# Opening stretch of a fused delta-rule attention and FFN kernel in a new layout

## The chip, the cores and the metric

One core of a Trainium2 chip. The metric is device time of one launch in microseconds (us), median of several runs. The engines are PE (matmul), DVE (vector), ACT (activations), POOL (general) and SP, which here only issues DMAs.

## What is computed

Two stages, one after the other in the reference:

```python
# attention: 4 batches, 8 heads, 768 tokens, head size 48
for t in range(S):
    kt, vt, bt = (k_n[:, :, t], v[:, :, t], beta[:, :, t, None])   # k_n: normalised k
    y[:, :, t] = np.einsum('bhd,bhde->bhe', q[:, :, t], state)
    v_old = np.einsum('bhde,bhd->bhe', state, kt)
    state = state + bt[:, :, :, None] * np.einsum('bhd,bhe->bhde', kt, vt - v_old)
# FFN on y as 3072 x 384, with w_in 384 x 2048 and w_out 2048 x 384
h = x @ w_in
sp = np.maximum(h, 0.0) + np.log1p(np.exp(-np.abs(h)))
g = h * erf(sp)
return (g @ w_out).astype(np.float32)
```

## The kernel before

**Attention.** Tokens are taken in 12 chunks c of 64. Per chunk: norms of k (norm_sq L197, norm_sum L205, norm_ops), a Gram matrix of k with itself ("pg", gram_mm L259, gram_a L269) and of q with k ("pq", gram_mm, gram_p L278 on ACT or L280 on DVE with the causal mask, gram_p2 L287 on POOL for the mask where gram_p was on ACT). For two chunks together (a pair, six of them) the triangular systems are solved in 32-by-32 blocks: the Gram matrix goes to DRAM (to_dram L294), back as blocks (to_blocks L303), 31 rows of two operations each (solve_row L320, L322; pair 0 on DVE, the others on POOL), then out and back again (put_blocks L327, from_blocks L334, from_blocks2 L342). The blocks are merged into whole inverses: merge_t (L349, DVE transposes), merge_e (L357), merge_e2 (L362), merge_z (L370), merge_z2 (L374), merge_m (L383), merge_m2 (L388 ACT, L390 DVE). The recurrence is a chain of 48 steps j = 4c + batch: load_v (L398), put_v (L405, POOL), chain_u (L418, PE), chain_u2 (L424, DVE), chain_s (L431), chain_s2 (L437 ACT or L439 DVE), chain_y (L445), chain_y2 (L454, ACT), chain_m (L458, DVE).

**FFN.** Four steps j make one of 12 token groups g (256 tokens). x is scaled and split into two fp16 halves (x_max to x_lo, L568 to L610). A group has 16 units: ffn1 (L622, nine matmuls 128x256 in fp16), and ffn2 (L677 to L679, six matmuls 128x384). Between them, two units at a time (u = 0 to 7): e_sp (L644, softplus on ACT), e_erf (L649, ACT), e_mul (L653, DVE), e_split (L660 ACT or L662 DVE), e_rest (L666, DVE or POOL). Softplus and erf have different tables on ACT, and each change is a table load (L139).

**Weights.** w_in and w_out come as float64 and are made into fp16 pairs on the chip, in 12 raw slices of 512 KB each: w_load (L490, SP), w_mask (L496, ACT), w_sign (L503, DVE), w_bits (L509 and L511, DVE), w_sum (L516, ACT), then for all slices w_max, w_all (PE), w_scale, and w_hi (L550, ACT) and w_lo (L559, DVE) in 16 parts each. Raw slices use the rooms ("H" and "L" tags) that the FFN's pairs use later.

**Room and order.** warm and fill (L154) are matmuls 128x384 on zeros: 15 at the start and WU single ones spread over the opening. early() (L122) lends w_out's room to tiles of the first pairs. PSUM: psa is a ring of three banks, pr is three banks, and "ph" and the warms have two. Every engine takes its instructions in order. Each step is put in a list with a planned time (on(), us(x), with constants such as C2, C3, MT, S1, WO that place chains, merges, solves and weights), the list is sorted by it, and then put in the order of ORDER, a tuple of indices written out (L33); so ORDER, not the planned times alone, sets each engine's queue. SP's queue holds loads, blocks and raw slices in one line, POOL's queue holds the solves, put_v, masks and half of e_rest.

Of the kernel before, what the change touches and what calls it, by code (L numbers as in the profile page):

```python
# [14 lines left out]
P = 128  # L15
# [19 lines left out]
MD = 4.4  # L35
CS = 1.2
WARM = 15
C2 = 2.0
C3 = 11.5
SS2 = 12.8  # L40
S1 = -2.5
SPL = 32
WG = -6
WU = 440
MT = 54
M1 = 0
# [36 lines left out]
@with_exitstack
def delta_ffn_kernel(ctx, tc, kT, qT, ktok, vtok, btok, w_in, w_out, cst, out):
# [151 lines left out]
    def norm_ops(sg, i, w=0):  # L236
        if i == 0:
            no[sg, w] = norms(sg, w)
        for fn in no[sg, w][i:i + 1] if sg < NSP else no[sg, w][3 * i:3 * i + 3]:
            fn()  # L240

    def load_kf(c, name):
        if c == 3 and name == "kpg":
            kf = early(5120, 1024).rearrange("p (a x) -> p a x", a=BP)
        else:
            kf = io.tile([P, BP, C], F32, tag="kf", bufs=3, name=f"{name}{c}")
        st[c][name] = kf
        for hb in range(2):
            sp.dma_start(kf[rd(hb)], kT[c, hb])
# [46 lines left out]
    def to_blocks(c):  # L296
        sg, i = divmod(c, 2)
        if i == 0:
            gb_t[sg] = at.tile([P, 32, 32], F32, tag="gb", name=f"gb{sg}") if sg else early(0, 1024).rearrange("p (a b) -> p a b", a=32)
        dv = st[c]["d1"].rearrange("(f s) h a t -> f (h a) s t", f=2)  # L300
        for f in range(2):
            q0 = i * 64 + f * 32
            sp.dma_start(gb_t[sg][q0:q0 + 32], dv[f, :, :, f * 32:f * 32 + 32])  # L303

    def solve_init(sg):
        xb_t[sg] = at.tile([P, 32, 32], F32, tag="xb", name=f"xb{sg}") if sg else early(1024, 1024).rearrange("p (a b) -> p a b", a=32)
        x = xb_t[sg].rearrange("p a b -> p (a b)")
        ge.memset(x, 0.0)
        ge.memset(x[:, ::33], 1.0)
# [426 lines left out]
    for i in range(WU):  # L736
        on(us(6 + 0.12 * i), fill)
# [212 lines left out]
```

## Time and profile before

| | us |
|---|---|
| runs of the kernel: median (lowest to highest of 3) | 709.91 (708.35 to 712.67) |
| the run that was profiled | 712.84 |
| span of the profiled execution | 711.1 |
| PE busy | 669.8 (94%) |
| ACT busy, of it table loads | 543.4 (76%), 237.4 |
| DVE busy | 435.9 (61%) |
| POOL busy | 332.3 (47%) |
| mean granted PE clock | 0.966 |

The span is counted from the first to the last instruction; the time of a run is a little longer. Engines work side by side, and a busy share is a mean over stretches with different limits.

### The profile page before, as it was taken

Reading aid. Unit: us, or ns where it says so; the run is one execution under the profiler, and the core shown is the slowest. Engines: PE = TensorE matmul, PEld = TensorE weight load, DVE = VectorE, ACT = ScalarE, POOL = GpSimd, SP = SyncE. Lnnn points to the kernel's source line nnn. Section 1 sums busy time; section 2 is a strip of 40 time slices with the busy share of each in tenths; the row PEclk is TensorE's granted clock in tenths of the full one; section 3 lists DMA queues with packets and bytes.
Section 4 is the critical chain, followed back from the end, with each engine's and each line's share of the span. In section 5 each row is a group of like instructions: output and inputs, shape, how many; then the busy total and the mean of one; then the engine's idle time right before and its main releaser. Section 6 shows DMA issues by size and latency. Waiting matters only on the chain.

```text
span 711.1 us, 22264 instructions
## 1 busy us (share of the span) xinstructions
PE 669.8 (94%) x9475; PEld 507.0 (71%) x9475; DVE 435.9 (61%) x1000; ACT 543.4 (76%) x767; POOL 332.3 (47%) x500
## 2 busy tenths in 40 slices
PE   7999997468999999999999999999999999999997
PEld 5666675356777787886878777877868777777764
DVE  3699859367896874777745659564564455534321
ACT  6214374378899999995994986967978969879993
POOL 4403999344201797898139751178831223201111
PEclk9999997577999999999999999999999999999999
DMA  9486541770004615713445114432041120000000
GB/s 244 105 257 209 166 126 42 210 173 14 3 2 109 152 38 120 159 42 93 85 91 135 35 33 96 101 81 64 18 97 29 26 63 7 24 1 13 12 23 22
DMA packets 87395, 59.05 MB, mean 83 GB/s; under 512 B 67776, under 2 KB 77120, under 8 KB 87296
## 3 DMA queue, kind: packets, MB, share of 16 engines
q1 hardware_dynamic: 87296, 57.63, 32.8%
q8 instruction: 74, 1.21, 0.7%
q14 instruction: 25, 0.20, 0.1%
HBM read 43.45 MB, written 14.16 MB: 81 GB/s over the span
## 4 chain that ended last, share of the span: by engine, by line
PE 67%; ACT 13%; DVE 5%; DMA 5%; issue 4%; POOL 3%; SPq 1%; POOLq 0%; ACTq 0%; DVEq 0%
PE ph L622 18%; PE warm L154 10%; ACT L139 7%; PE pr L677 6%; PE pr L679 6%; PE pr L678 6%; PE pg L259 3%; PE pc L445 3%; PE pc L418 3%; PE pq L259 2%; PE pm L383 2%; DMA k<-ktok 2%; PE pc L431 2%; ACT L L649 2%; ACT L L644 2%
## 5 line engine op out<-in xcount | busy, mean ns | idle before, releaser
L139 ACT ACT_TABLE_LOAD x185 | 237.4, 1283 | 4.0 <-PEq L943 0.7
L622 PE MATMUL ph<-xh,w_in 128*128 128x256 f16 x1152 | 204.2, 274 | 4.2 <-DVE L L653 3.9
L622 PEld LDWEIGHTS <-w_in 128*128 128x128 f16 x1728 | 165.9, 98 | 32.3 <-DVE L L653 4.4
L666 POOL TENSOR_TENSOR H<-L,H 128x512 f16<-128x512 f32 x58 | 67.0, 1157 | 242.9 <-DVE H L662 154.9
L622 PE MATMUL ph<-xl,w_in 128*128 128x256 f16 x576 | 157.4, 273 | 0.0
L653 DVE SCALAR_TENSOR_TENSOR L<-ph,L 128x512 f32<-128x512 f32 x96 | 66.1, 689 | 114.4 <-ACT L L649 107.6
L677 PE MATMUL pr<-w_out,H 128*128 128x384 f16 x384 | 126.0, 328 | 0.0
L679 PE MATMUL pr<-w_out,H 128*128 128x384 f16 x384 | 125.6, 327 | 0.0
L678 PE MATMUL pr<-w_out,H 128*128 128x384 f16 x384 | 125.6, 327 | 0.0
L320 POOL TENSOR_TENSOR tmptmpg<-gb,xb 128x31 f32<-128x31 f32 (+15 forms) x155 | 88.8, 573 | 51.1 <-DMA gb<-d 42.0
L322 POOL TENSOR_TENSOR xb<-xb,tmptmpg 128x31 f32<-128x31 f32 (+15 forms) x155 | 88.6, 571 | 12.1
L644 ACT ACTIVATE L<-ph,xct 128x512 f32<-128x512 f32 x96 | 65.8, 687 | 21.6 <-POOL z L405 9.1
L154 PE MATMUL warm<-zero 128*128 128x384 f16 x455 | 80.2, 337 | 1.1 <-DVE zero L145 1.1
L405 POOL TENSOR_TENSOR z<-v,nm 64x192 f32<-64x192 f32 x96 | 58.5, 609 | 28.8 <-DMA v<-vtok 22.0
L154 PEld LDWEIGHTS <-zero 128*128 128x128 f16 x455 | 44.6, 100 | 31.8 <-issue 3.6
L649 ACT ACTIVATE L<-L 128x512 f32<-128x512 f32 x96 | 60.4, 629 | 1.1
L679 PEld LDWEIGHTS <-H 128*128 128x128 f16 x384 | 37.7, 98 | 25.1 <-issue 0.3
L677 PEld LDWEIGHTS <-H 128*128 128x128 f16 x384 | 37.6, 98 | 20.8 <-issue 0.2
L678 PEld LDWEIGHTS <-H 128*128 128x128 f16 x384 | 37.7, 98 | 18.6 <-issue 0.2
L666 DVE TENSOR_TENSOR H<-L,H 128x512 f16<-128x512 f32 x38 | 28.1, 740 | 25.9 <-ACT H L660 25.8
L424 DVE TENSOR_TENSOR z<-pc,ga 64x192 f32<-64x192 f32 x88 | 31.2, 355 | 17.7 <-PE pc L418 15.3
L259 PE MATMUL pq<-qp,kpq 48*64 48x64 f32 x640 | 25.4, 238 | 16.8 <-DMA qp<-qT 16.8
(138 smaller groups left out, 961.6 us busy)
## 6 DMA issues: line engine op xcount, KB each, us to landing
raw_in<-w_in SPq DMA_DIRECT2D x12, 512.0 KB, 7.6
raw_out<-w_out SPq DMA_DIRECT2D x12, 512.0 KB, 4.8
d<-A SPq DMA_DIRECT2D x20, 256.0 KB, 3.1
k<-ktok SPq DMA_DIRECT2D x12, 384.0 KB, 4.0
qp<-qT SPq DMA_DIRECT2D x24, 192.0 KB, 3.5
v<-vtok SPq DMA_DIRECT2D x48, 96.0 KB, 2.9
out<-ob SPq DMA_DIRECT2D x48, 96.0 KB, 2.2
kpg<-kT SPq DMA_DIRECT2D x22, 192.0 KB, 5.0
```

Source lines behind the costliest of these rows:

```text
L139: se.add_instruction(mybir.InstLoadActFuncSet(name=nc.get_next_instruction_name(), act_func_set_id=i, ins=[], outs=[]))
L154: te.matmul(wp[0], zero[:, :P], zero, start=True, stop=True)
L320: eng.tensor_tensor(tv, G[:, s, s + 1:].unsqueeze(1).broadcast_to([P, ncol, nr]), Xv[:, :, s:s + 1].broadcast_to([P, ncol, nr]), op=ALU.mult)
L322: eng.tensor_tensor(Xv[:, :, s + 1:], Xv[:, :, s + 1:], tv, op=ALU.add)
L622: te.matmul(ph, w[:, i, kt * P:kt * P + P], G[x][:, :, ksl], start=(m == 0), stop=(m == 8))
L644: se.activation(unit(g, u), G["ph", u], AF.Softplus, bias=0.0, scale=G["ct"])
L649: se.activation(Lu, Lu, AF.Erf, bias=0.0, scale=1.0)
L653: ve.scalar_tensor_tensor(Lu, fg[g]["ph", u], HSC, Lu, op0=ALU.mult, op1=ALU.mult)
L666: (ve if u % (2 if g < GLE else GLM) == 0 else ge).tensor_tensor(G["gl", u], unit(g, u), G["gh", u], op=ALU.subtract)
L677: te.matmul(G["po"][a], gh[:, o, asl], wout_h[:, i, :], start=(i == 0), stop=False)
L678: te.matmul(G["po"][a], gh[:, o, asl], wout_l[:, i, :], start=False, stop=False)
L679: te.matmul(G["po"][a], gl[:, o, asl], wout_h[:, i, :], start=False, stop=(i == NFF - 1))
```

## The change

The work is the same; its place in time and its rooms change.

- The second solve (chunks 2 and 3) is planned from us(76) to us(116) in place of us(30) to S1, and with it go later: loads and norms of the pair, its grams (the second half-gram of chunk 2 stands behind the warms), to_dram. Merges are planned from MT = 58 (54), the chains of chunks 2 and 3 from C2 = 12 (2) and C3 = 16 (11.5).
- w_in's slices 0 to 5 are loaded right behind the first loads, and masked, signed and made into bits ahead of solve 0; slices 6 to 11 within and behind it.
- w_out's slices are planned one by one (WOT): 0 to 3 within solve 0, 6, 10 and 11 next, then 4, 5, 7, 8, 9. Before, all came from WO in steps of 0.4.
- q of chunks 0 and 1 is loaded behind to_blocks; v of the first six steps early.
- WU is 390 (440). In the new order 32 warms stand ahead of the grams of chunk 0, 109 ahead of the pq grams, 235 ahead of half-gram 2 1, one ahead of w_all and merge_e 0, and none later.
- HB, the rooms for pairs and raw slices of tag "H", is 7 (6). The early() rooms of chunk 3's gram input, chunk 3's A, and the first solve's two tiles are gone: they now come from their own pools.
- S2A is empty: chain_s2 of steps 0 to 3 is on DVE (an addition) and not on ACT (a copy). CP and CM are (2, 3): gram_p of chunks 0 and 1 is on DVE with the mask in it (no POOL step), and half of the merge copies of chunks 0 and 1 are on DVE.
- e_split of groups 0 and 1 is all on ACT (before, and in later groups, units 0, 2, 4, 6).
- ORDER is new throughout. On DVE from half-gram 2 1 on: gram_a 2 1, merge_t 0, w_scale, merge_t 1, then w_lo spread between merge copies, gram_p, chain and bit operations, to x_lo 0 1. On PE: merge_e 0 and 1, merge_z 0 and 1, grams 3, chain steps and merge_m of chunk 1, pq grams 2, x_tr, ffn1 0 behind chain_y 6.

```diff
--- before.py
+++ after.py
@@ -30,28 +30,26 @@
 RW = 512
 HALF = BP // 2
 
...
 LEAD = 3
 MD = 4.4
 CS = 1.2
 WARM = 15
-C2 = 2.0
-C3 = 11.5
+C2 = 12.0
+C3 = 16.0
 SS2 = 12.8
 S1 = -2.5
 SPL = 32
 WG = -6
-WU = 440
-MT = 54
+WU = 390
+MT = 58
 M1 = 0
-WL = (1, 25, 25.1, 25.2, 25.3, 25.4, 25.5, 25.6, 26, 26.1, 26.2, 26.3)
-WK = (14, 27, 28, 29, 30, 31, 32, 33, 34, 35, 36, 37)
-WF = (14.5, 42.02, 42.03, 42.04, 42.05, 42.06, 43, 44, 45, 46, 47, 48)
-WI = (20, 47.2, 48.2, 49.4, 52, 54, 56, 58, 60, 62, 64, 66)
-WO = -4.1
+WL = (0.9, 0.95, 1.0, 1.05, 1.1, 1.15, 24, 24.1, 31.0, 32.5, 34.0, 35.5)
+WK = (6.0, 6.7, 7.4, 8.1, 8.8, 9.5, 28, 29, 36.0, 37.5, 39.0, 40.5)
+WF = (6.6, 7.3, 8.0, 8.7, 9.4, 10.1, 28.6, 29.6, 36.6, 38.1, 39.6, 41.1)
+WI = (17.0, 18.0, 19.0, 20.0, 21.0, 22.0, 31, 32, 50.5, 52.1, 53.7, 55.3)
+WOT = (36, 38, 40, 42, 76, 78, 62, 86, 88, 90, 72, 74)
 WD = 0.4
-SGI = ()
-SGO = ()
 RI = "HLHLHLHLHLHH"
 RO = "H" * 12
 LMI = [0] * 16
@@ -60,7 +58,7 @@
 LOD = 0.25
 SPA = (0, 2, 4, 6)
 EB = 2
-HB, LB = 6, 5
+HB, LB = 7, 5
 GLE = 7
 GLM = 4
 PA, PB = 3, 3
@@ -68,9 +66,9 @@
 NSP = 0
 XR = 3
 YR = 6
-S2A = (0, 1, 2, 3)
-CP = (0, 1, 2, 3)
-CM = (0,1,2,3)
+S2A = ()
+CP = (2, 3)
+CM = (2, 3)
 FB = 6.9
 T0 = 82.0
 SW = 4.6
@@ -190,7 +188,7 @@
 
     def norm_sq(c):
         s = st[c]
-        if c < 4:
+        if c < 2:
             s["sq"] = ff.tile([P, BP, D], F32, tag="L", bufs=LB, name=f"sq{c}")
         else:
             s["sq"] = at.tile([P, BP, C], F32, tag="A", name=f"sq{c}")[:, :, :D]
@@ -236,14 +234,11 @@
     def norm_ops(sg, i, w=0):
         if i == 0:
             no[sg, w] = norms(sg, w)
-        for fn in no[sg, w][i:i + 1] if sg < NSP else no[sg, w][3 * i:3 * i + 3]:
+        for fn in no[sg, w][3 * i:3 * i + 3]:
             fn()
 
     def load_kf(c, name):
-        if c == 3 and name == "kpg":
-            kf = early(5120, 1024).rearrange("p (a x) -> p a x", a=BP)
-        else:
-            kf = io.tile([P, BP, C], F32, tag="kf", bufs=3, name=f"{name}{c}")
+        kf = io.tile([P, BP, C], F32, tag="kf", bufs=3, name=f"{name}{c}")
         st[c][name] = kf
         for hb in range(2):
             sp.dma_start(kf[rd(hb)], kT[c, hb])
@@ -261,8 +256,8 @@
     def gram_a(c, i):
         s = st[c]
         if i == 0:
-            if c in (1, 3):
-                s["A"] = early(1024 * (1 + (c + 1) // 2), 1024).rearrange("p (a x) -> p a x", a=BP)
+            if c == 1:
+                s["A"] = early(2048, 1024).rearrange("p (a x) -> p a x", a=BP)
             else:
                 s["A"] = at.tile([P, BP, C], F32, tag="A", name=f"A{c}")
         hs = slice(i * HALF, i * HALF + HALF)
@@ -296,14 +291,14 @@
     def to_blocks(c):
         sg, i = divmod(c, 2)
         if i == 0:
-            gb_t[sg] = at.tile([P, 32, 32], F32, tag="gb", name=f"gb{sg}") if sg else early(0, 1024).rearrange("p (a b) -> p a b", a=32)
+            gb_t[sg] = at.tile([P, 32, 32], F32, tag="gb", name=f"gb{sg}")
         dv = st[c]["d1"].rearrange("(f s) h a t -> f (h a) s t", f=2)
         for f in range(2):
             q0 = i * 64 + f * 32
             sp.dma_start(gb_t[sg][q0:q0 + 32], dv[f, :, :, f * 32:f * 32 + 32])
 
     def solve_init(sg):
-        xb_t[sg] = at.tile([P, 32, 32], F32, tag="xb", name=f"xb{sg}") if sg else early(1024, 1024).rearrange("p (a b) -> p a b", a=32)
+        xb_t[sg] = at.tile([P, 32, 32], F32, tag="xb", name=f"xb{sg}")
         x = xb_t[sg].rearrange("p a b -> p (a b)")
         ge.memset(x, 0.0)
         ge.memset(x[:, ::33], 1.0)
@@ -497,10 +492,7 @@
 
     def w_sign(nm, i):
         hi = wt[nm]["raw", i][:, :, 1]
-        if i in (SGI if nm == "in" else SGO):
-            ge.tensor_scalar(hi, hi.bitcast(F32), 0.0, -2.0 ** 31, op0=ALU.is_lt, op1=ALU.mult)
-        else:
-            ve.tensor_scalar(hi, hi, -0x80000000, None, op0=ALU.bitwise_and)
+        ve.tensor_scalar(hi, hi, -0x80000000, None, op0=ALU.bitwise_and)
 
     def w_bits(nm, i, k):
         raw = wt[nm]["raw", i]
@@ -656,7 +648,7 @@
         G = fg[g]
         pr_ = pair(g, u)
         G["gh", u], G["gl", u] = pr_[:, 0], pr_[:, 1]
-        if (g * NFF // EU + u) % 8 in SPA:
+        if g < 2 or u in SPA:
             se.copy(G["gh", u], unit(g, u))
         else:
             ve.tensor_copy(G["gh", u], unit(g, u))
@@ -708,8 +700,8 @@
         return chain_at(c * B) - MD * (0.65 if c == 2 else 1) if c > 1 else us(MT)
 
     NSG = NC_ // 2
-    solve_end = [us(42), S1] + [chain_at(2 * sg * B) - MD - 1.3 for sg in range(2, NSG)]
-    solve_start = [us(22), us(30), SS2] + [solve_end[sg - 1] + 1.3 for sg in range(3, NSG)]
+    solve_end = [us(50), us(116)] + [chain_at(2 * sg * B) - MD - 1.3 for sg in range(2, NSG)]
+    solve_start = [us(28), us(76), SS2] + [solve_end[sg - 1] + 1.3 for sg in range(3, NSG)]
 
     def gram(t, d, c, name):
 
@@ -734,17 +726,19 @@
     on(-99, clear_second)
     on(-98, warm, WARM)
     for i in range(WU):
-        on(us(6 + 0.12 * i), fill)
+        on(us(6 + 0.17 * i), fill)
     on(us(0), clear_q)
-    for i, (fn, *a) in enumerate(((load_step, 0), (load_step, 1), (load_beta, 0), (load_kf, 0, "kpg"), (load_kf, 1, "kpg"), (load_q, 0), (load_q, 1),
+    for i, (fn, *a) in enumerate(((load_step, 0), (load_step, 1), (load_beta, 0), (load_kf, 0, "kpg"), (load_kf, 1, "kpg"),
                                   (load_cst,))):
         on(us(0.1 + 0.05 * i), fn, *a)
     on(us(6.5), clear_x)
+    on(us(19), load_q, 0)
+    on(us(21), load_q, 1)
     for sg in range(2):
-        t = (4, 10.5)[sg]
+        t = (4, 20)[sg]
         if sg:
             for i, (fn, a) in enumerate(((load_step, 2), (load_step, 3), (load_beta, 1))):
-                on(us(0.6 + 0.05 * i), fn, a)
+                on(us(14 + 0.05 * i), fn, a)
         for x in range(2):
             on(us(t + 1.1 * x), norm_sq, 2 * sg + x)
             on(us(t + 1.1 * x + (0.2 if sg == 0 else 1.0)), norm_sum, 2 * sg + x)
@@ -754,25 +748,24 @@
                     on(us(5.5 + 0.9 * w + 0.22 * i), norm_ops, sg, i, w)
         else:
             for i in range(6):
-                on(us((6.4, 13.4)[sg] + 0.4 * i), norm_ops, sg, i)
+                on(us((6.4, 24)[sg] + 0.3 * i), norm_ops, sg, i)
     for c in range(4):
-        t = (5.5, 8, 12.2, 15)[c]
-        ta = (10.6, 12, 16.3, 18)[c]
+        t = (5.5, 8, 63.2, 65.2)[c]
+        ta = (10.6, 12, 64, 66)[c]
         for i in range(2):
             on(us(t + 1.3 * i), gram_mm, c, i, "pg")
             on(us(ta + 0.6 * i), gram_a, c, i)
-        on(us((11.9, 13.3, 17.6, 19.3)[c]), to_dram, c)
+        on(us((11.9, 13.3, 66, 68)[c]), to_dram, c)
     on(us(14), to_blocks, 0)
     on(us(14.1), to_blocks, 1)
     on(us(1), solve_init, 0)
-    on(us(0.8), load_kf, 2, "kpg")
-    on(us(0.85), load_kf, 3, "kpg")
+    on(us(30), load_kf, 2, "kpg")
+    on(us(30.5), load_kf, 3, "kpg")
     for c in range(2):
         for i in range(2):
-            t = 20.8 + 2.5 * (2 * c + i)
+            t = (56, 57, 71.5, 73)[2 * c + i]
             on(us(t), gram_mm, c, i, "pq")
-            on(us(t + 2.6), gram_p, c, i)
-            on(us(24.6 + 2.5 * (2 * c + i)), gram_p2, c, i)
+            on(us((64, 65, 72.7, 74.2)[2 * c + i]), gram_p, c, i)
 
     for sg in range(NSG):
         t0, t1 = solve_start[sg], solve_end[sg]
@@ -807,8 +800,8 @@
                     on(tq + 0.6 + 0.9 * i, gram_p2, c, i)
         else:
             tm = [us(MT + x + 1.25 * c) for x in (0, 1.2, 2.2, 3.6, 4.8, 6, 7.2, 7.3, 8.5)]
-            on(us(22 + c), from_blocks, c)
-            on(us(42.4 + 0.2 * c), from_blocks2, c)
+            on(us(30 + c), from_blocks, c)
+            on(us(50.4 + 0.2 * c), from_blocks2, c)
             if c == 1:
                 tm = [us(MT + M1 + x) for x in (1.2, 2.4, 3.4, 4.8, 6, 10.5, 11.7, 11.8, 13)]
         on(tm[0], merge_t, c)
@@ -826,8 +819,8 @@
     for j in range(B * NC_):
         t = chain_at(j)
         d = 1.0 if j >= 2 * B else 2.6 / SW / CS
-        on(t - 3.3 if j >= 2 * B else t - us(4) + us(0), load_v, j)
-        on(t - 1.2 if j >= 2 * B else t - us(2) + us(0), put_v, j)
+        on(t - 3.3 if j >= 2 * B else us(32 + 2 * j) if j < 6 else t - us(6) + us(0), load_v, j)
+        on(t - 1.2 if j >= 2 * B else us(52 + 1.3 * j) if j < 6 else t - us(2) + us(0), put_v, j)
         on(t, chain_u, j)
         on(t + 0.2 * d, chain_u2, j)
         if j < B * NC_ - B:
@@ -846,14 +839,14 @@
             on(us(tb + 0.8 * k), w_bits, "in", i, k)
         on(us(tb + 2.4), w_sum, "in", i)
     for i in range(NRW):
-        t = WO + WD * i
+        t = us(WOT[i])
         on(t - 0.9, w_load, "out", w_out.bitcast(I32), i, RO[i])
         on(t - 0.3, w_mask, "out", i)
         on(t - 0.2, w_sign, "out", i)
         for k in range(2):
             on(t + 0.15 * k, w_bits, "out", i, k)
         on(t + 0.5, w_sum, "out", i)
-    for nm, t in (("in", us(WI[-1] + 3)), ("out", WO + WD * (NRW - 1) + 1.2)):
+    for nm, t in (("in", us(WI[-1] + 3)), ("out", us(max(WOT)) + 1.2)):
         on(t, w_max, nm)
         on(t + 0.05, w_all, nm)
         on(t + 0.15, w_scale, nm)
```

## Rows read from the trace of the kernel before

**Rows 1.** Busy time by stretch; PEclk is PE's granted clock.
```profile
core 0: us, PE busy (x) PEld busy (x) DVE busy (x) ACT busy (x) POOL busy (x), PEclk, DMA share, GB/s
...
84.00:115.00 31.00, 29.67 (x675) 21.80 (x674) 20.73 (x40) 21.30 (x50) 28.83 (x35) 1.00 0.42 119
115.00:145.00 30.00, 16.55 (x220) 13.43 (x216) 15.92 (x44) 13.29 (x27) 17.39 (x27) 0.60 0.57 147
...
75.00:125.00 50.00, 45.19 (x806) 31.99 (x803) 39.03 (x82) 28.49 (x68) 45.95 (x60) 0.92 0.36 109
...
289.00:711.00 422.00, 412.45 (x5941) 317.10 (x5934) 231.03 (x529) 346.01 (x446) 183.70 (x289) 1.00 0.24 55
```

**Rows 2.** Timeline of PE (start, duration, line, tiles, count, idle before).
```profile
10.75 3.32 PE L154 MATMUL warm<-zero 128*128 128x384 f16 x11
...
37.35 46.65 PE L154 MATMUL warm<-zero 128*128 128x384 f16 x286
83.93 1.20 PE L357 MATMUL pe<-T,A 32*32 32x32 f32 x64
...
99.13 0.67 PE L418 MATMUL pr<-z,xm 128*64 128x48 f32 x16
...
119.44 1.09 PE L418 MATMUL pc<-z,xm 128*64 128x48 f32 x16 [0.59 <-DVE xm L575]
...
134.94 4.12 PE L259 MATMUL pq<-qp,kpq 48*64 48x64 f32 x64 [10.59 <-DMA qp<-qT]
...
162.25 0.28 PE L622 MATMUL ph<-xh,w_in 128*128 128x256 f16 x1
...
163.47 0.38 PE L622 MATMUL ph<-xh,w_in 128*128 128x256 f16 x2
```

**Rows 3.** Timeline of DVE in the opening stretch.
```profile
38.08 0.18 DVE L320 TENSOR_TENSOR tmpT<-w_out 128x31 f32<-128x31 f32 x1
...
53.01 0.68 DVE L509 SCALAR_TENSOR_TENSOR w_in<-w_in,raw_in 128x512 int32<-128x512 int32 x1
53.61 0.40 DVE L320 TENSOR_TENSOR tmpT<-w_out 128x240 f32<-128x240 f32 x1
...
75.87 1.43 DVE L349 STREAM_TRANSPOSE T<-xm 32x512 f32<-32x512 f32 x2
...
123.78 1.08 DVE L610 SCALAR_TENSOR_TENSOR xl<-pt,xsx,xh 128x256 f16<-128x256 f32 x3
```

**Rows 4.** Instructions by line and form on DVE: count, busy us, mean ns.
```profile
L424 DVE TENSOR_TENSOR z<-pc,ga 64x192 f32<-64x192 f32 x88 | 31.2, 355 | 17.7 <-PE pc L418 15.3
...
L280 DVE TENSOR_TENSOR qp<-pq,mask 64x512 f32<-64x512 f32 x32 | 22.0, 688 | 3.3 <-PE pq L259 2.7
...
L559 DVE SCALAR_TENSOR_TENSOR w_in<-w_in,sc_in 128x384 f16<-128x384 f32 x16 | 10.3, 641 | 17.1 <-ACT w_in L550 16.9
```

**Rows 5.** Timeline of SP's DMA queue.
```profile
66.12 1.09 SPq L327 DMA_DIRECT2D d<-w_out  x2
...
126.19 1.09 SPq L327 DMA_DIRECT2D d<-xb  x2
```

**Rows 6.** Timeline of POOL: first and last operation of two solves.
```profile
64.28 0.48 POOL L320 TENSOR_TENSOR tmptmpg<-gb,xb 128x31 f32<-128x31 f32 x1 [37.37 <-DMA gb<-d]
...
125.90 0.27 POOL L322 TENSOR_TENSOR xb<-xb,tmptmpg 128x31 f32<-128x31 f32 x1
...
233.29 0.24 POOL L320 TENSOR_TENSOR tmptmpg<-gb,xb 128x31 f32<-128x31 f32 x1 [1.83 <-DMA gb<-d]
...
274.95 0.27 POOL L322 TENSOR_TENSOR xb<-xb,tmptmpg 128x31 f32<-128x31 f32 x1
```

**Rows 7.** Timeline of ACT: table load and two softplus.
```profile
140.94 1.28 ACT L139 ACT_TABLE_LOAD   x1
142.24 0.69 ACT L644 ACTIVATE L<-ph,xct 128x512 f32<-128x512 f32 x1
...
289.13 0.69 ACT L644 ACTIVATE L<-ph,xct 128x512 f32<-128x512 f32 x1
```

2 lines of the change are left out of this document (1 added, 1 removed).

## Prediction

> **What bounds the kernel now.** I read four views in this order: the busy table by stretch, TensorE's (PE's) timeline, then the timelines of the engines that release it, and last the two softplus instructions that cut the run into parts.
>
> By stretches [rows 1]: from 289 us on PE is busy 412.45 of 422 us at clock 1.00, so 59% of the span is PE work and falls only if PE has less left to do. The stretch 115 to 145 is the weak one: PE 16.55 of 30 us, DVE 15.92, ACT 13.29, POOL 17.39, granted clock 0.60. Nobody is full there.
>
> PE's timeline [rows 2]: 286 warm matmuls fill 37.35 to 84.0 (0.163 us each), and the merge of chunk 0 follows at once at 83.93. A full engine here is a wait in disguise: the first solve on DVE starts at 38.08 [rows 3], and its blocks go out at 66.12 [rows 5]. At 134.94 PE has waited 10.59 us for a load of q. That load is queued on SP behind the put_blocks at 126.19 [rows 5], which wait for the second solve on POOL, 64.28 to 126.17 (the first and the last of 62 operations, [rows 6]). So a POOL solve holds up a load that has nothing to do with it. The first softplus, at 142.24, is the end of the opening stretch; the first of group 3, at 289.13, is where PE becomes the bound [rows 7].
>
> I cut the time at those two: opening 142.2, middle 146.9, rest 421.9 (711.1 minus 289.13). The run that was profiled took 712.84, so 1.7 lie around the span, and it is 0.4% above the median, 709.91. I sum in its frame and scale at the end.
>
> **Opening, to the merge of chunk 0.** Only the norms and grams of chunks 0 and 1 stand ahead of solve 0 now, but 12 bit operations for w_in slices 0 to 5, six w_sign, and the second pair's norms (18 short operations) do too. The list ahead of the solve ends at about 36, near the 38.08 of before [rows 3]. The solve itself carries 22 weight operations (10 w_sign, 12 w_bits; before: 19), so it ends at about 70 to 72.5, and merge_t could follow 10 us later as before (blocks put at 66.12, merge_t at 75.87 [rows 3, 5]), at 80 to 82. PE is later than that. Eleven warms at 10.75 took 3.32 us at the lower clock [rows 2]; 32 of them and three grams end near 20.7 (an estimate, 18 to 24). Then 109 x 0.163 = 17.8, the four pq grams 3.9, seven warms 1.1, one gram 1.0, 235 x 0.163 = 38.3: 82.8. Only then comes gram 2 1, and DVE's gram_a 2 1 waits for it, with both merge_t queued behind. So merge_t 0 is at 84.6 and merge_e 0 at about 86.5, against 83.93. Fewer warms (390 for 440) buy nothing here: the loss is 2.5, and if solve 0 ends later than 72.5 it is that which counts.
>
> **Opening, from there to the first softplus.** DVE holds the list: from gram_a 2 1 to x_lo 0 1 about 101 instructions. 16 w_lo at 0.641 are 10.3; 15 of 512 columns (3 gram_a; 6 gram_p of chunks 0 and 1, now with the mask on DVE; 6 merge copies, now half on DVE) at 0.688 are 10.3; 32 of the chain (14 chain_u2, 12 chain_s2, of which 8 come from ACT, 6 chain_m) at 0.355 are 11.4 [rows 4]; 10 w_bits at 0.68 are 6.8; 6 x_lo are 2.2 [rows 3]; 4 transposes and 5 w_sign, bounded by 0.688, 6.2; 13 small ones at 0.2, 2.6. Together 49.8. Starts follow one another up to 0.08 before the end of the instruction ahead (53.01 plus 0.68, next at 53.61 [rows 3]), so 42 at least; I take 45. The waits are the unknown: before, 75 to 125 held the same kind of work with 39.03 of 50 busy [rows 1], 11 of wait; I take 10. From 83.9: 138.9. Two ffn1 units and the table load stand between x_lo and softplus: 3.2, as from 139.06 to 142.24. First softplus at **142.1**, where it was. The 10.59 of before are gone (chunk 2's q is loaded long before solve 1 ends), but the w_lo, gram_p and bit work that lay beside them is now in line.
>
> The cost of no warms is in this too: after merge_e 0 the new order has none. A chain_u took 0.67 among warms (99.13) and 1.09 without (119.44) [rows 2]. PE's work to the first ffn1 is about 25 us at full clock, 50 at half, in a stretch of 53: hidden if it alternates well with DVE, and not if it doesn't.
>
> The Trainium skill, "TensorE: Matmul & The Clock Gate", section "A second HAM failure mode: psum-queue depth-cycling", describes PE pausing between bursts while it cycles through PSUM banks and so falling back to the lower clock, at a cost in throughput. The trace agrees: 0.60 in 115 to 145, where there are no warms, and 1.00 in 84 to 115, where there are [rows 1]. By that rule the stretch would run at the 1.2 GHz level, which is the first rival below.
>
> **Middle, first softplus to group 3's.** I sum PE and ACT in the new order between the softplus of units 0 0, 0 4, 1 0, 2 0 and 3 0, with ffn1 at nine times 0.111 (162.25 to 163.47, 11 matmuls), ffn2 at six times 0.163, and a table load of 1.28 at each change [rows 2, 7]. The larger of the two: ACT 26, ACT 20.5, PE 57 (chains 8 to 15 and four merge_m moved here, ACT 50), ACT 39.5, together 143. Before by the same sums: 38, 25, 39, 34, 136, which took 146.9, so 11 of stalls. The 57 is 16 ffn1 (16.0), 16 ffn2 (15.7), eight chain steps at 1.69 (13.5), five grams (4.9), four merge_m (3.8), a merge_e and a merge_z (2.2) and the transposes of x (1.2). The eight e_split that come to ACT in groups 0 and 1 are in ACT's sums. Stalls that I see: load_q 3 waits for chain_y 7, and gram 3 0 pq for it ahead of ffn1 4, about 4. Solve 1 now starts at about 115: by the second solve of before it takes 61.9, by the third 41.9 (233.29 to 275.22) [rows 6]; I take 52, and 12 more to the merge, 179. PE is at merge_e 2 near 185, so no stall, but 4 late by the long price. Solve 2 against merge_e 4: 0 to 4. I take 8: 151.
>
> **Rest.** At that softplus PE is 9 us further in the new order: 3 ffn2 units (2.9), two chain_u and one chain_s and chain_y (2.3), a merge_e and a merge_z (2.2), two merge_m (1.9). In a stretch that is PE's own this is worth its full 9: 421.9 - 9.3 = 412.6. The seventh H room only covers a wait for a room; split work of ACT against DVE is off the path here.
>
> **Sum.** 142.1 + 151 + 412.6 = 705.7; with 1.7, 707.4; times 709.91/712.84, **704.5**.
>
> **Rivals.**
> - *Half clock takes the opening* (slower). PE at its lower level and the three PSUM banks make DVE wait at every chain step. The row for it: 115 to 145, without warms, DVE share 0.53 [rows 1]. By it 45/0.53 = 85, first softplus 172, sum 736, run 734. It decides as soon as DVE's share falls under about 0.66 (45/0.66 = 68 for 55), which is also just the 0.67 of 84 to 115, a stretch with warms. Against it: in 115 to 145 a third of the stretch is the one wait for q, which goes.
> - *The gain is given back* (no change). Solve 1 goes at the slow price and merge_e 2 comes 4 late, or the 57 of PE in group 1 is at less than full clock; 5 more: 709.
> - *DVE hardly waits* (more gain). w_lo and w_bits are spread through the list so that DVE always has work: 4 of wait, softplus at 134 to 136, stalls 4: 693.
>
> **How the numbers follow.** Forecast as summed, 698 to 710: 0.42. Hardly any wait, 686 to 698: 0.19. Given back, 706 to 714: 0.17. Half clock, 714 to 736: 0.22. About 1% is what a measurement can tell from no change: under 702.8 is faster, over 717.0 slower. Faster: all of the third rival and half of the forecast's 0.42, 0.40. Slower: nearly all of the first rival, 0.21. Within 1%: 0.39. Range 688 to 722, which leaves out the worst half of the half-clock case and the best end of the other; the forecast alone is 698 to 710.
>
> **What would show it.** gram_a 2 1 on DVE waiting for PE near 84 shows the opening right. DVE busy at least 0.8 from there to x_lo 0 1, and a softplus at 140 to 144, show the list; a share under 0.66 with a clock near 0.5 to 0.6 shows the first rival. No wait of PE for q before ffn1. In the middle, a first merge_e 2 that follows ffn1 without a wait shows solve 1 in time. From group 3's first softplus to the end 412 to 413, if PE is that much further; a rest of 422 would make that step wrong.

## The result

The changed kernel takes 705.82 us (median of 13 runs, 702.92 to 706.95), the kernel before 712.24 in the same comparison (13 runs, 707.75 to 713.52): a ratio of 0.9908, with an interval of 0.9887 to 0.9928. The forecast was 704.5 against 709.91, a ratio of 0.9924. The profiled execution has a span of 704.9 for 711.1.

Busy time by stretch of the kernel after: merge of chunk 0 to x_lo, then between the first softplus of groups 0, 1, 2 and 3, then to the end (answering to [rows 1]).

```profile
core 0: us, PE busy (x) PEld busy (x) DVE busy (x) ACT busy (x) POOL busy (x), PEclk, DMA share, GB/s
...
85.00:137.10 52.10, 36.44 (x798) 33.00 (x798) 44.85 (x102) 28.24 (x57) 17.00 (x25) 0.64 0.67 174
...
140.70:190.50 49.80, 42.95 (x561) 33.21 (x561) 42.31 (x84) 45.28 (x69) 42.86 (x59) 0.90 0.23 51
...
190.50:249.30 58.80, 57.95 (x1041) 45.14 (x1040) 40.60 (x99) 48.78 (x74) 40.16 (x69) 1.00 0.33 76
...
249.30:289.90 40.60, 40.39 (x560) 30.89 (x559) 25.11 (x50) 39.11 (x50) 24.05 (x46) 1.00 0.63 136
...
289.90:704.90 415.00, 405.64 (x5731) 313.49 (x5729) 227.98 (x518) 348.07 (x443) 171.93 (x268) 1.00 0.23 51
```

The same view of the kernel before, its last stretch from its first softplus of group 3:

```profile
285.20:711.10 425.90, 416.25 (x6002) 320.10 (x5999) 232.90 (x532) 349.76 (x449) 186.95 (x297) 1.00 0.24 56
```

Timeline of PE after ([rows 2]): the long block of warms, half-gram 2 1, merge_e 0, the first ffn1, merge_e 2.

```profile
45.52 38.36 PE L152 MATMUL warm<-zero 128*128 128x384 f16 x235
...
83.81 1.15 PE L254 MATMUL pg<-kpg 48*64 48x64 f32 x32
...
87.41 1.20 PE L352 MATMUL pe<-T,A 32*32 32x32 f32 x64 [1.17 <-DVE m_in L520]
...
137.00 0.40 PE L614 MATMUL ph<-xh,w_in 128*128 128x256 f16 x1
...
184.68 1.20 PE L352 MATMUL pe<-T,A 32*32 32x32 f32 x64
```

Timeline of DVE after ([rows 3]): first and last operation of solve 0, gram_a 2 1, merge_t 0, x_lo 0 1.

```profile
37.41 0.19 DVE L315 TENSOR_TENSOR tmpT<-gb,xb 128x31 f32<-128x31 f32 x1
...
75.02 0.22 DVE L317 TENSOR_TENSOR xb<-xb,tmpT 128x31 f32<-128x31 f32 x1
...
85.00 0.69 DVE L264 TENSOR_TENSOR A<-pg,gn 128x512 f32<-128x512 f32 x1 [2.37 <-PE pg L254]
...
85.61 1.42 DVE L344 STREAM_TRANSPOSE T<-xm 32x512 f32<-32x512 f32 x2
...
135.98 1.08 DVE L602 SCALAR_TENSOR_TENSOR xl<-pt,xsx,xh 128x256 f16<-128x256 f32 x3
```

SP's queue ([rows 5]): put_blocks of solve 0, from_blocks2, load_q 2, put_blocks of solve 1. Load_q 2 stands 55.6 us ahead of the put_blocks that it stood behind.

```profile
75.26 1.09 SPq L322 DMA_DIRECT2D d<-xb  x2
...
78.36 4.51 SPq L337 DMA_DIRECT2D xm<-d  x8
...
118.28 0.84 SPq L187 DMA_DIRECT2D qp<-qT  x2
...
173.88 1.09 SPq L322 DMA_DIRECT2D d<-xb  x2
```

POOL ([rows 6]): first and last row of solve 1, 54 us.

```profile
119.75 0.76 POOL L315 TENSOR_TENSOR tmptmpg<-gb,xb 128x31 f32<-128x31 f32 x1 [5.17 <-DMA gb<-d]
...
173.59 0.27 POOL L317 TENSOR_TENSOR xb<-xb,tmptmpg 128x31 f32<-128x31 f32 x1
```

ACT ([rows 7]): the first softplus of group 0 and that of group 3.

```profile
140.74 0.69 ACT L636 ACTIVATE L<-ph,xct 128x512 f32<-128x512 f32 x1 [2.01 <-PE ph L614]
...
289.90 0.69 ACT L636 ACTIVATE L<-ph,xct 128x512 f32<-128x512 f32 x1
```

And of the kernel before the softplus of group 3, which the forecast had taken from the wrong row:

```profile
285.19 0.69 ACT L644 ACTIVATE L<-ph,xct 128x512 f32<-128x512 f32 x1
```

285.19 is group 3's first; 289.13, used in the forecast, is its second (two softplus stand in one line of the timeline further up, as x2, and were taken for one). With the right row the three parts are:

| part | before | after | forecast for after |
|---|---|---|---|
| opening, to the first softplus | 142.2 | 140.7 | 142.1 |
| middle, to group 3's | 143.0 | 149.2 | 151 |
| rest, to the end | 425.9 | 415.0 | 412.6 |

So the opening brings 1.5 us, the middle costs 6.2, and the rest gives 10.9. The two windows above show why the rest is shorter: PE is busy 405.64 us there for 416.25. It isn't faster, it has 10.6 us less left to do. Counted by line, the two windows differ by the steps that the forecast named: 32 matmuls of chain_u, 16 each of chain_s and chain_y, 64 each of merge_e, merge_z and merge_m, and 15 of ffn2 (three units are 18).

### The profile page after: what moved, and what is told of

Its sections match the earlier page's. It is cut to its first block, busy times and chain, and to the rows that moved or that the text cites. A ratio compares the mean times of both kernels' runs of the same rounds, so it can differ in the third digit from the quotient of the medians.

```text
span 704.9 us, 22114 instructions
## 1 busy us (share of the span) xinstructions
PE 668.5 (95%) x9425; PEld 509.2 (72%) x9425; DVE 448.5 (64%) x1014; ACT 544.5 (77%) x755; POOL 313.0 (44%) x492
## 4 chain that ended last, share of the span: by engine, by line
PE 60%; DVE 15%; ACT 14%; issue 4%; DMA 4%; SPq 2%; POOL 1%; POOLq 0%; ACTq 0%; DVEq 0%
PE ph L614 19%; ACT L137 7%; PE pr L669 6%; PE pr L671 6%; PE pr L670 6%; PE warm L152 3%; PE pm L378 3%; PE pc L440 3%; PE pq L254 3%; PE pc L413 3%; PE pg L254 3%; ACT L L636 2%; ACT L L641 2%; PE pc L426 2%; PE pe L352 2%
## 5 line engine op out<-in xcount | busy, mean ns | idle before, releaser
L614 PE MATMUL ph<-xh,w_in 128*128 128x256 f16 x1152 | 219.9, 276 | 2.0 <-DVE L L645 1.7
L671 PE MATMUL pr<-w_out,H 128*128 128x384 f16 x384 | 125.6, 327 | 0.7 <-POOL H L658 0.7
L315 POOL TENSOR_TENSOR tmptmpg<-gb,xb 128x31 f32<-128x31 f32 (+15 forms) x155 | 85.4, 551 | 24.7 <-DMA gb<-d 15.8
L400 POOL TENSOR_TENSOR z<-v,nm 64x192 f32<-64x192 f32 x96 | 51.9, 540 | 96.9 <-DVE raw_in L495 37.4
L152 PE MATMUL warm<-zero 128*128 128x384 f16 x405 | 71.0, 339 | 1.1 <-DVE zero L143 1.1
L152 PEld LDWEIGHTS <-zero 128*128 128x128 f16 x405 | 40.5, 101 | 29.6 <-issue 4.1
L652 ACT CAST H<-L 128x512 f16<-128x512 f32 x56 | 34.3, 613 | 14.8 <-DVE L L645 14.7
L434 DVE TENSOR_TENSOR z<-pc,z 48x192 f32<-48x192 f32 x80 | 28.4, 355 | 24.4 <-PE pc L440 19.3
```

The costliest lines, as they stand in the source:

```text
L152: te.matmul(wp[0], zero[:, :P], zero, start=True, stop=True)
L315: eng.tensor_tensor(tv, G[:, s, s + 1:].unsqueeze(1).broadcast_to([P, ncol, nr]), Xv[:, :, s:s + 1].broadcast_to([P, ncol, nr]), op=ALU.mult)
L614: te.matmul(ph, w[:, i, kt * P:kt * P + P], G[x][:, :, ksl], start=(m == 0), stop=(m == 8))
L671: te.matmul(G["po"][a], gl[:, o, asl], wout_h[:, i, :], start=False, stop=(i == NFF - 1))
```

## The experiments

All times in the table are from one profile of each kernel: its first softplus, the lengths of middle and rest; beside them the ratio to the kernel before with its interval. Single profiles of kernels that are alike up to the merges differ by up to 2.4 us in where the first softplus falls (140.3 in a_split_old, 142.7 in a_hb6), so a shift of 2 us there says nothing; the lengths of the rest agree within 3 among kernels of one order. Nor is the profiled run always a typical one: it took 2.8 us more than the median in b_q_early, 2.4 in a_24_more and a_act_copies. The intervals of the ratios are 1.5 to 4.2 us to either side.

| kernel | first softplus | middle | rest | ratio |
|---|---|---|---|---|
| before | 142.2 | 143.0 | 425.9 | 1 |
| b_q_early | 141.4 | 143.9 | 425.4 | 0.9960 (0.9929 to 0.9991) |
| b_raw_early | 142.3 | 139.4 | 426.2 | 0.9957 (0.9927 to 0.9987) |
| b_q_raw_early | 134.2 | 143.3 | 425.5 | 0.9884 (0.9824 to 0.9943) |
| b_q23_raw_early | 133.1 | 144.0 | 426.2 | 0.9870 (0.9830 to 0.9910) |
| changed | 140.7 | 149.2 | 415.0 | 0.9908 (0.9887 to 0.9928) |
| a_24_more | 147.3 | 147.7 | 415.5 | 0.9961 (0.9934 to 0.9989) |
| a_fill_gap | 139.5 | 148.1 | 416.3 | 0.9938 (0.9905 to 0.9972) |
| a_late_warms | 140.8 | 149.8 | 414.4 | 0.9920 (0.9881 to 0.9960) |
| a_act_copies | 141.8 | 147.9 | 415.2 | 0.9895 (0.9862 to 0.9928) |
| a_wlo_pool | 143.7 | 147.9 | 413.9 | 0.9918 (0.9889 to 0.9947) |
| a_split_old | 140.3 | 149.2 | 413.7 | 0.9926 (0.9900 to 0.9953) |
| a_hb6 | 142.7 | 148.8 | 414.1 | 0.9904 (0.9865 to 0.9943) |
| a_pq3_late | 142.4 | 153.9 | 413.7 | 0.9990 (0.9966 to 1.0013) |

Kernels b_ start from the kernel before, kernels a_ from the changed one. Where steps are moved, on() also keeps the step's name, ix() finds a step by it, and the list is edited behind the line that applies ORDER.

**What was the price of the old opening?** Four kernels make a square: chunk 2's q early or not, w_out's raw slices 8 to 11 early or not.

```diff
# b_q_early
+    e = ev.pop(ix("load_q", 2))
+    ev.insert(ix("chain_y", 3) + 1, e)
```

> The kernel before with one step moved: the load of chunk 2's q stands behind chain_y 3 in SP's queue and no longer behind the put_blocks of the second solve. Theory (the wait for q was the price of the old opening, and a gain in the opening goes through to the end): the 10.59 us wait of PE goes, the first softplus comes 8 to 12 us earlier than 142.2, the merge of chunk 2 then waits some 5 us for the second solve, and the total falls by 4 to 8 us against before. Rival (the wait covered for work that ACT and DVE had to do anyway): softplus moves by less than 4 and the total by less than 2.

In the opening the rival came out: the softplus moves by 0.9 us. The total is 2.9 us less (0.6 to 5.1), between the two forecasts. SP's queue of this kernel, load_q 2, put_blocks, and the raw slice behind them:

```profile
109.96 0.79 SPq L189 DMA_DIRECT2D qp<-qT  x2
...
127.63 1.10 SPq L327 DMA_DIRECT2D d<-xb  x2
...
128.82 0.54 SPq L490 DMA_DIRECT2D raw_out<-w_out  x1
```

and ACT's timeline, w_mask, the w_hi queued behind it, and the first softplus:

```profile
134.73 0.66 ACT L496 ACTIVATE w_out<-raw_out 128x512 f32<-128x512 f32 x1 [9.33 <-DMA raw_out<-w_out]
...
135.29 0.60 ACT L550 ACTIVATE w_in<-w_in,sc_in 128x384 f16<-128x384 f32 x1
...
141.36 0.69 ACT L644 ACTIVATE L<-ph,xct 128x512 f32<-128x512 f32 x1
```

The q is there at 110 and PE's wait for it is gone, but w_mask now waits 9.33 us for a slice of w_out whose load is issued at 128.82, behind the same put_blocks. w_hi of w_in stands behind w_mask on ACT, w_lo behind that, ffn1 behind that. The kernel before had this wait all along; ACT's waits there, 110 to 145 us (total, times, longest):

```profile
ACT w_out L496 <- DMA raw_out<-w_out: 14.6, 3, 10.1
```

The Trainium skill, "TensorE: Matmul & The Clock Gate", section "Architectural detail: the array is 16× 32×32, not 1× 128×128", gives ScalarE and VectorE strictly first-in first-out queues. The trace agrees: w_hi starts at 135.29, right behind the w_mask that waited, though the last w_lo ahead of it had ended at 125.6; DVE's next w_lo waited 9.12 us for it.

```diff
# b_q_raw_early
+    for a, b in ((("load_q", 2), ("chain_y", 3)),) + tuple((("w_load", "out", i), ("w_sum", "out", i - 6)) for i in (8, 9, 10, 11)):
+        e = ev.pop(next(i for i, e in enumerate(ev) if e[3] == a or e[3][:2] + e[3][3:4] == a))
+        ev.insert(max(ix("chain_y", 3), ix(*b)) + 1, e)
```

(w_sum of slice i - 6 is the last reader of the room that slice i takes.)

> The kernel before with q of chunk 2 and also w_out's raw slices 8 to 11 ahead of the put_blocks of the second solve in SP's queue. With q alone the first softplus moved by 0.9 us, because ACT's w_mask of slice 8 waited 9.33 us for its load behind the same put_blocks, and w_hi, w_lo and ffn1 behind it. Theory (the queue behind the second solve is the price of the old opening): now the first ffn1 follows at 128 to 131, softplus at 131 to 134 for 142.2; the merge of chunk 2, which does need the solve (ended at 126, back at 135), holds PE for some 5 us; total 3 to 7 us less than before. Rival (the opening is held by other work, and the order of merges takes all of it back): total within 2 us of before.

SP's queue of it, load_q 2, the last slices, put_blocks:

```profile
112.07 1.87 SPq L189 DMA_DIRECT2D qp<-qT  x2
...
114.04 1.50 SPq L490 DMA_DIRECT2D raw_out<-w_out  x3
...
128.81 1.09 SPq L327 DMA_DIRECT2D d<-xb  x2
```

PE of it, the pq grams of chunk 2, merge_e 2, and those of chunk 3:

```profile
126.64 3.68 PE L259 MATMUL pq<-qp,kpq 48*64 48x64 f32 x64
...
138.87 1.20 PE L357 MATMUL pe<-T,A 32*32 32x32 f32 x64
...
149.21 0.44 PE L259 MATMUL pq<-qp,kpq 48*64 48x64 f32 x2 [6.67 <-DMA qp<-qT]
```

The softplus comes 8 us earlier, and all of it reaches the end of this profile: middle and rest are as long as before. The 5 us wait of the merge didn't come, since merge_e 2 runs at 138.87 behind ffn1 without one. Five load steps moved in the old order thus give 0.9884, the whole change 0.9908; the intervals overlap, and neither can be called faster.

```diff
# b_raw_early: as above without load_q 2
```

> The kernel before with only w_out's raw slices 8 to 11 ahead of the put_blocks of the second solve; q of chunk 2 stays behind them. It completes the square of four: neither early 142.2 for the first softplus, q alone 141.4, both 134.2. Theory (two waits side by side behind the same queue entry, so that taking either alone gives nothing): PE still waits for q until about 135, softplus within 1.5 us of 142.2, total within 3 us of before. Rival (the raw slices alone were the price): softplus at 136 or earlier, total 5 to 8 us under before.

PE's waits of it, 85 to 145 us, and put_blocks in SP's queue:

```profile
PE pq L259 <- DMA qp<-qT: 9.0, 2, 8.6
```

```profile
127.65 1.09 SPq L327 DMA_DIRECT2D d<-xb  x2
```

Theory: with the slices alone the softplus stays. The 0.4% that the kernel gains comes in the middle (139.4); its cause was not followed up. There w_mask had waited only 0.6 us, while PE's wait for chunk 3's pq gram falls from 6.2 to 3.5.

For the opening it is a joint wait, which neither load ends alone. It shows best from the put_blocks of the second solve, whose own time differs between the four profiles (126.19, 127.63, 127.65, 128.81): the softplus follows 16.1 us behind it in the kernel before, 13.7 with q early, 14.7 with the slices early, 5.4 with both. The totals by themselves don't show it: 2.9 and 3.1 us less alone, 8.3 (4.1 to 12.5) together.

```diff
# b_q23_raw_early: as b_q_raw_early, and
+    for a, b in ((("load_q", 3), ("chain_y", 7)), (("load_v", 10), ("load_q", 3)), (("gram_mm", 3, 0, "pq"), ("ffn1", 5)),
+                 (("gram_mm", 3, 1, "pq"), ("gram_mm", 3, 0, "pq")), (("gram_p", 3, 0), ("gram_mm", 3, 0, "pq")), (("gram_p2", 3, 0), ("gram_p", 3, 0))):
+        e = ev.pop(ix(*a))
+        ev.insert(ix(*b) + 1, e)
```

> The kernel before with q of chunk 2 and the raw slices 8 to 11 early, as in the run before, and also chunk 3's q loaded right behind chain_y 7 and its pq grams behind ffn1 5, since PE waited 7.3 us for that q at 142 to 150. Theory (both loads were late only by their place in SP's queue, and what PE has in hand by the middle is worth its time to the end): the wait goes, group 3's first softplus 2 to 6 us earlier than 277.4, total 9 to 13 us under before, so 4 to 7 under the changed kernel. Rival (ACT bounds 134 to 277, and PE's wait there is free): group 3's softplus within 1.5 us of 277.4, total 6 to 9 under before, as without it.

By group 3's softplus (277.1) it is the rival: PE's wait for q goes, and middle and rest stay (144.0, 426.2). In its place PE waits 2.9, 2.2 and 1.7 us for other things before 160 us. The total, 9.3 us under before (6.4 to 12.1), can't tell the two apart, and that ACT bounds the stretch, as the rival says, isn't shown. Of the waits of PE that the views list, this one was free; the one at 134.94 was half of a joint one.

**Does a shift of the opening reach the end?**

```diff
# a_24_more
+    i = ix("gram_mm", 2, 1, "pg")
+    ev[i:i] = [(0, 0, fill, ("fill",))] * 24
```

> The changed kernel with 24 warms more ahead of half-gram 2 1 (24 x 0.163 = 3.9 us). Theory (the warms set gram_a 2 1, and a shift of the opening goes through the middle to the end): softplus 3.9 later, and the total 3 to 4 us more than the changed kernel. Rival (the middle, bound by ACT and by waits, takes up a shift of the opening): softplus later by 3.9, total by less than 1.5.

It does: the ratio is 0.0053 higher, 3.8 us, for 3.9 us of warms, though the two intervals together leave 1.4 to 6.2. In the profile merge_e 0 comes 3.9 us later (91.35), as summed; the softplus comes 6.6 later, more than the warms explain, and 5.6 of that is in the span.

**What sets the opening of the changed kernel?**

```diff
# a_fill_gap
+    i = ix("gram_mm", 2, 1, "pg")
+    w = [n for n in range(i) if ev[n][3] == ("fill",)][-24:]
+    ev = [e for n, e in enumerate(ev) if n not in w]
+    for k in (("w_all", "in"), ("w_scale", "in"), ("w_hi", "in", 0, 0), ("w_lo", "in", 0, 0), ("gram_p", 0, 1)):
+        e = ev.pop(ix(*k))
+        ev.insert(ix("merge_t", 0), e)
```

> The changed kernel with 24 warms fewer ahead of half-gram 2 1 (3.9 us), and w_scale, one w_lo and one gram_p put ahead of merge_t 0 on DVE, where DVE waits 2.4 us. Theory (warms and the blocks of solve 0 end level, so merge_t stays at 85 to 86, but 2 to 3 us of DVE's list go into the gap, and DVE's list sets the stretch to 101): softplus 1.5 to 3 us earlier than 140.7, total 1 to 3 us less than the changed kernel. Rival A (the warms alone set it): merge_t at 82, softplus 4 earlier. Rival B (the chain from step 0 on sets the end, whatever DVE does before): no change within 1 us.

PE's waits of it, 85 to 145 us:

```profile
PE pe L352 <- DVE T L344: 4.9, 2, 4.5
```

DVE's timeline of it, the moved gram_p and merge_t 0:

```profile
84.43 1.39 DVE L275 TENSOR_TENSOR qp<-pr,mask 64x512 f32<-64x512 f32 x2
85.74 1.42 DVE L344 STREAM_TRANSPOSE T<-xm 32x512 f32<-32x512 f32 x2
```

Merge_t stays at 85.7, and PE waits 4.5 us for it. But merge_t follows the moved gram_p without a wait: it is the work put ahead of it that holds it. The last load of solve 0's blocks was issued at 81.0, and these loads took 1.9 to 2.6 us, so by that the blocks were there near 83. So the run doesn't decide rival A, and how close warms and solve end is told by the changed kernel alone. Softplus moves by 1.3, and the total doesn't get less (0.9938), which is rival B as far as it can be told.

```diff
# a_late_warms
+    for n, k in ((10, ("merge_e", 1)), (10, ("merge_z", 0)), (4, ("gram_mm", 3, 0, "pg")), (4, ("chain_u", 0)),
+                 (4, ("merge_m", 1, 0)), (4, ("chain_u", 3)), (6, ("chain_s", 3)), (4, ("chain_u", 4)), (14, ("chain_s", 4)),
+                 (4, ("chain_u", 5)), (6, ("chain_s", 5)), (8, ("chain_s", 6))):
+        i = ix(*k)
+        ev[i:i] = [(0, 0, fill, ("fill",))] * n
```

> The changed kernel with 78 warm matmuls put back between the merges and the first chain steps, where PE waits. Rival of the forecast (PE at the lower clock holds the opening back): granted clock rises from 0.64 to 0.9 or more in 85 to 137 us, DVE's 7 us of waits shrink to 3 or less, first softplus at 137 or earlier, total 3 to 4 us less than the changed kernel. Theory (DVE's list of 45 us sets it, with 7 us of waits that are mostly waits for dependences): the clock rises too, but softplus stays within 1.5 us of 140.7 and the total within 1.5 us of the changed kernel.

The window of it from 85 to 137.1 us:

```profile
85.00:137.10 52.10, 43.03 (x842) 30.73 (x840) 42.16 (x95) 27.81 (x57) 18.42 (x28) 0.87 0.64 166
```

The clock rises from 0.64 to 0.87, and the softplus is at 140.8 for 140.7. So these warms buy nothing. That the lower clock is free doesn't follow. Counted from gram_a 2 1, chain_s of step 4 comes 35.8 us after it (119.70) for 37.1 in the changed kernel (122.14), so up to there the higher clock brings 1.4 us. Then it is lost: ACT waits for a raw slice, and ten of the warms stand ahead of chain_u and chain_s of step 5.

```profile
121.90 0.67 ACT L491 ACTIVATE w_out<-raw_out 128x512 f32<-128x512 f32 x1 [2.38 <-DMA raw_out<-w_out]
...
125.27 1.46 PE L152 MATMUL warm<-zero 128*128 128x384 f16 x4
...
130.32 2.03 PE L152 MATMUL warm<-zero 128*128 128x384 f16 x6
```

From gram_a 2 1 to x_lo 0 1 DVE has the same 44.8 us to do, in 54.8 us for 52.1: its waits don't shrink to 3, they grow from 7.2 to 10.0.

```diff
# a_act_copies
-S2A = ()
-CM = (2, 3)
+S2A = (0, 1, 2, 3)
+CM = (0, 1, 2, 3)
```

> The changed kernel with the merge copies of chunks 0 and 1 and chain_s2 of steps 0 to 3 back on ACT: 6 instructions of 0.68 and 8 of 0.355 leave DVE, 7 us of its 44.85 in 85 to 137 us; ACT, busy 28 of 52 there, takes them. Theory (DVE's list sets the opening): first softplus 3 to 6 us earlier than 140.7, and as a gain there goes through to the end, total 2 to 5 us less than the changed kernel. Rival (the chain's and merges' own latency sets it, or ACT becomes late with w_hi): softplus within 1.5 us, total within 1.5 us.

The same window of it, and a part of its chain of waits:

```profile
85.00:137.10 52.10, 33.66 (x807) 30.19 (x801) 40.03 (x87) 33.02 (x71) 17.72 (x27) 0.68 0.66 173
```

```profile
109.19 7.17 DMA raw_out<-w_out
...
116.39 0.67 ACT w_out L491
...
117.06 0.52 ACT w_in L542
```

```diff
# a_wlo_pool
-LMI = [0] * 16
+LMI = [1] * 8 + [0] * 8
```

> The changed kernel with w_lo of w_in's parts 0 to 7 on POOL, idle until 119 us, in place of DVE: 8 x 0.6 = 4.9 us leave DVE, ACT gets 8 activations of 0.6 more. Theory (DVE's list sets the stretch 85 to 101, the chain's latency the rest): the first chain_u 2 to 3 us earlier than 101.7, softplus 1 to 3 earlier, total 1 to 3 less than the changed kernel. Rival (the list is full of waits that only move, as with the copies on ACT): softplus within 1 us, total within 1.

The same window of this kernel:

```profile
85.00:137.10 52.10, 36.60 (x789) 33.16 (x785) 38.70 (x84) 31.12 (x60) 22.38 (x31) 0.61 0.66 170
```

In both the rival came out. From gram_a 2 1 to x_lo 0 1 DVE is busy 40.0 of 51.6 us and 41.7 of 54.5, for 44.8 of 52.1, and the softplus is no earlier. The work that leaves the list turns into waits, in the first for a raw slice (7.17 us from issue to w_mask, then w_hi, w_lo, and the chain behind them). In the changed kernel the chain of waits runs through POOL at that place, where put_v stands between rows of solve 1:

```profile
123.92 0.50 POOL z L400
...
124.50 0.50 POOL z L400
...
125.00 0.79 POOL tmptmpg L315
...
127.09 0.36 DVE z L419
```

Added up from 86.4 to 137.1 us, that chain has 22.7 us on DVE, 21.1 on PE, much of it at the lower clock, 3.0 on POOL and 1.9 on ACT; its first 11 us are nearly all DVE. So DVE's list has a part in the opening, but doesn't set it alone; and the work taken from DVE came to stand on ACT and POOL in the same stretch, so the two runs don't show what the opening would be without it. I read this as several chains of nearly one length; no run shortens two of them together. None of the four kernels shortened the opening by more than 1.3 us.

**The parts that were forecast as free.**

```diff
# a_split_old
-        if g < 2 or u in SPA:
+        if u in SPA:
# a_hb6
-HB, LB = 7, 5
+HB, LB = 6, 5
```

> The changed kernel with e_split of groups 0 and 1 divided as before between ACT and DVE (units 0, 2, 4, 6 on ACT). ACT loses 8 x 0.61 = 4.9 us in the middle, DVE gets 8 x 0.47. Theory (from 190 to 249 us PE is the bound of the middle with 57 of 59 us, and ACT only in the short stretches): group 3's first softplus within 2 us of 289.9, total within 1.5 us of the changed kernel. Rival (ACT bounds the middle): 3 to 5 us less.

> The changed kernel with six H rooms for seven. Theory (a wait for a room is covered, as the forecast says): total within 1.5 us of the changed kernel. Rival (raw slices and pairs of groups 0 and 1 wait for rooms, in the opening or between 190 and 250 us): 2 to 6 us more.

Both came out as the theory says, as far as intervals of some 3 us can tell: 0.9926 and 0.9904 for 0.9908, and group 3's softplus at 289.5 and 291.5 for 289.9.

```diff
# a_pq3_late
+    for a, b in ((("gram_mm", 3, 0, "pq"), ("ffn1", 5)), (("gram_p", 3, 0), ("gram_mm", 3, 0, "pq"))):
+        e = ev.pop(ix(*a))
+        ev.insert(ix(*b) + 1, e)
```

> The changed kernel with half-gram 3 0 pq behind ffn1 5, where its q has arrived; PE waited 3.3 us for it ahead of ffn1 4. Theory (that wait is one of the stalls of the middle, as summed in the forecast): total 1 to 3 us less than the changed kernel. Rival (ACT, busy 45 of 50 us between the softplus of groups 0 and 1, bounds that stretch): group 1's softplus within 1 us of 190.5, total within 1.

Neither: it is 0.8% slower. PE's waits, 140 to 200 us, of the changed kernel and then of this one:

```profile
PE pq L254 <- issue: 2.9, 1, 2.9
...
PE pq L254 <- DMA qp<-qT: 0.4, 1, 0.4
```

```profile
PE sp L475 <- DVE xm L560: 3.7, 1, 3.7
```

The 3.3 us are gone, and PE comes to x_all 1 before DVE has reached x_max 1, which stands behind the bit operations of w_out: 3.7 us there, and the middle is 4.7 longer. Why it costs more than it saves was not followed further; the ring of three PSUM banks is taken in another order too.

## Why the forecast was right, point by point

- **Total and direction**: 0.9924 forecast, 0.9908 measured.
- **merge_e 0**: 86.5 forecast, 87.41. The warms do end at 83.81, and DVE waits 2.37 us for half-gram 2 1. But the cover was thinner than said: solve 0 ended at 75.24, not 70 to 72.5 (it starts 1.4 later, waits 1.74 for w_mask of a raw slice, and some rows took longer). The last load of its blocks was issued at 82.4, and these took 2.0 to 2.9 us, so they were back at 84.4 to 85.3 by that, level with gram_a 2 1 at 85.00. The mis-sized term is solve 0, by 3 to 5 us.
- **DVE's list**: 45 us forecast, 44.85; waits 10, 7.25; x_lo done at 138.9, 137.06; softplus 142.1, 140.74. The sum is right, the reading of it only in part: with 5 and 3 us less for DVE to do (a_act_copies, a_wlo_pool) the opening was no shorter, so DVE's list doesn't set it alone, for all that DVE was 86% busy there. Over two fifths of the chain of waits is PE (21.1 us of 50.7), whose work the forecast took as hidden if it alternates well with DVE.
- **The wait for q**: that it goes was right. That it alone was the price of the old opening was wrong: ACT's 10.1 us wait for a raw slice of w_out stood beside it, behind the same put_blocks. The forecast read only PE's releaser. This didn't spoil the sum, since the new opening was summed from its own list.
- **Half clock** (rival, 0.22): the clock did fall to 0.64, DVE's share was 0.86, far over the 0.66 from which it was to decide, and a_late_warms gained nothing by raising the clock. What the lower clock costs by itself stays open: a merge_e takes 1.92 us at it (92.36) for 1.20 (87.41), and such steps are in the chain of waits, but the warms that raise the clock take PE's time too. The rule of the Trainium skill that the prediction names ("TensorE: Matmul & The Clock Gate", section "A second HAM failure mode: psum-queue depth-cycling") fits the clock. That the pauses come from the PSUM banks no run shows.
- **Middle**: sum of stages 143 and 8 of stalls, 149.2 measured, so 6. Group 1's stretch took 58.8 for 57, PE 57.95 of it at clock 1.00. merge_e 2 was forecast near 185 without a stall, and runs at 184.68; solve 1 took 54 us for 52.
- **Rest**: 9.3 less, 10.9 measured (PE 10.6). This step is right, and by the steps that it named. In level it is 412.6 against 415.0, because 421.9 starts at the wrong row: from the right one it is 425.9 - 9.3 = 416.6.
- **Sum**: the stages of the middle (151) end at group 3's first softplus, the rest starts at its second, so the 3.9 us between are in no part. Put right, the sum is 709.7 and the forecast 708.5 for 704.5. That the span came out at 704.9 for 705.7 is thus in part luck: opening, middle and rest (416.6) are each 1.4 to 1.8 us too long, 4.8 together, and the lost 3.9 us hide it. The row also made the stalls of before 11 us, where they were 7.

What the change does is then this: it takes q and the raw slices out from behind the second solve, and it has 10.6 us of PE work of chains, merges and ffn2 done ahead of group 3's softplus, in a middle that grows by 6.2. Beside the old order with the same queue freed (b_q_raw_early) its rest is 10.5 us shorter, its opening 6.5 longer (140.7 against 134.2) and its middle 5.9 longer: the new order as a whole has no gain beyond that of the five load steps that a measurement here can tell. Which of its chains must be cut to get the opening back stays open, and no run takes the moved PE work alone.

## What to carry to other kernels

When an engine waits long for a load, list everything that stands behind the same entry of that queue, and look at the waits of all engines in that stretch: here two loads behind one put_blocks each hid the other, and only moving both brought the first softplus 8 us forward. Cut a trace at two or three milestones, and count what the bound engine has left to do at each: a shift of the opening went through to the end nearly whole (8 us in b_q_raw_early, 5.6 of 6.6 in the profile of a_24_more). Work done earlier shortens what comes behind by its full length (10.9 us for 10.6), but what it costs where it lands has to be set against that (6.2 here). And add up the parts from the same rows: a milestone read from two rows lost 3.9 us here. A busy share of 86% is no proof that an engine is the bound; taking work from it is a better test, as long as that work doesn't come to stand in the same chain on another engine.

## What the runs showed that was not expected

PE at a granted clock of 0.64 for 52 us, against 0.87 with 78 more matmuls on zeros in the same stretch, made no difference to the first softplus (140.7 and 140.8): filling matmuls raise the clock, but stand on the path themselves, and here the two were level. And the same code up to the merges put merge_e 0 anywhere from 83.7 to 86.5 us in five profiles of the old order, so one profile can't tell shifts of 2 us in an opening. It begins with the first matmuls: in the new order the 32 warms ahead of chunk 0's grams took 5.38 us in a_split_old and 7.33 in a_act_copies, and merge_e 0 came at 84.17 and 87.93.
